# A hand-written planner counts small products for half of TensorE's load and lets blocks of TensorE instructions come later

## The chip, the cores and the metric

The kernel runs on one core of a Trainium2 chip. The metric is device time in microseconds (us) of one execution, the median of several. Engines are named as in the profile: PE (TensorE matmuls), PEld (its weight loads), DVE (VectorE), ACT (ScalarE), POOL (GpSimd), SP (the queue that issues the transfers).

## The reference, cut to what matters

Three stages follow each other on 4 batches of 768 tokens: a gated recurrent attention (8 heads of 40), a token mixer whose weights are a 768 x 768 matrix pair, and a gated convolution.

```
for t in range(S):                                   # attention, S = 768
    m_new = maximum(f_gate + m, i_gate); f_stab, i_stab = exp(f_gate+m-m_new), exp(i_gate-m_new)
    C = f_stab * C + i_stab * outer(v, k);  n = f_stab * n + i_stab * k
    y[t] = sigmoid(o_gate) * (C @ q) / maximum(abs(n @ q), 1)
theta = x @ w_theta                                  # x: y as (4, 768, 320)
y = w_tok_r @ (x * cos(theta)) + w_tok_i @ (x * sin(theta))
u = x + y;  x2 = u + maximum(u @ w_ch, 0)
out = (sigmoid(conv5(x2)) * (x2 @ w_val)) @ w_out
```

## The kernel before

**Attention** works in 12 groups g of two chunks of 128 tokens (`attend`, once per group). On PE a group is `weigh` (28 bf16 matmuls that build the decay exponents in two banks of PSUM; ACT takes their Exp into a tile W), `scores` (k by q, in the same two banks; DVE multiplies them into W), `carry` (twice 32, the state's update), `numer` (64, W by v) and `inter` (64, state by q). A float32 matmul counts as two PE matmuls, each with its weight load, so a group has 284. Their outputs are 41, 64 or 128 to 512 columns wide. `finish` on DVE divides and applies the output gate, whose Sigmoid (`sig`, tiles `x_m`) runs on ACT for two groups at a time. Exp, Sigmoid and Sin need different tables on ACT, so a change of function costs an `ACT_TABLE_LOAD`.

**The mixer and the convolution** are 24 steps. `theta` makes x @ w_theta and its sine and cosine for 128 tokens (tiles `th_m`, `z`); `weight` converts one block of the token matrix (tiles `r_b`, `wt_m`); `mix` adds 30 products of 384 columns per block; the `f_...` functions are the rest. `theta` for the first 128 tokens comes in the program between the last groups of attention, because it takes the same two banks.

**Conversions.** The dense weights come as float64 bit patterns, and `cv_piece` turns each of 13 pieces (three each of w_theta, w_ch, w_val and w_out, and the convolution's) into float32: one Abs on ACT, then four operations on DVE in place in `xT_m` (`cv_bits`: two TENSOR_SCALAR, two SCALAR_TENSOR_TENSOR), then a split into a high and a low part (`out_hi`, `out_lo`, `val_hi`, `val_lo`) on ACT and on DVE or POOL. Nothing needs the w_val and w_out pieces before the convolution stage.

**The order of the work** is not the program's. Every call is recorded as a step of a `Plan`, with engines that may do it and a cost for each; `order` then simulates the engines and takes, whenever an engine is free, the ready step that is due first. For PE it keeps a model of the clock and of the instruction stream (`array`): time is cut into windows, the share of work in a window switches the modelled clock between half and full speed (to full above WARM, back to half below COLD), and every BLOCK = 127 matmuls a new block of instructions begins, no earlier than FETCH us after the block before it began. `issue` runs `order` four times, each time with PE's due times taken from the run before, keeps the run that its own model ends first, and records the instructions in that order. Each engine then runs its list strictly in that order.

Of the kernel before, what the change touches and what calls it, by code (L numbers as in the profile page):

```python
# [72 lines left out]
class Plan:  # L73
# [8 lines left out]
    LATE, AGAIN, BESIDE = -2.5, 4, 0.5  # L82
    HOP, TABLE, HOLD = 0.15, 1.3, 5.0
    WINDOW, PHASE, WARM, COLD = 3.413, 0.6, 0.85, 0.45
    BLOCK, FETCH = 127, 3.6
    DMA_ISSUE, DMA_START, DMA_END, DMA_RATE, DMA_DEPTH = 0.475, 0.65, 0.95, 260e3, 8

    def __init__(self, nc):
# [108 lines left out]
    def order(self, aim=None):  # L197
        steps, after = self.steps, self.edges()
# [26 lines left out]
        def array(n, t):  # L225


            nonlocal slow, window, worked, used, block
            cost, todo = steps[n]["cost"]["pe"], steps[n]["ninst"]
            load, each = min(1.0, steps[n]["work"] / cost), cost / todo  # L230
            while todo:
                some = min(todo, self.BLOCK - used)
                left = some * each
                while left > 1e-6:
                    w = int((t + self.PHASE + 1e-6) / self.WINDOW)
                    for _ in range(window, w):
                        share, worked = worked / self.WINDOW, 0.0
                        slow = share < (self.WARM if slow else self.COLD)
                    window = w
                    rate = 0.5 if slow else 1.0  # L240
                    span = min(left / rate, (w + 1) * self.WINDOW - self.PHASE - t)
                    left -= span * rate
                    worked += span * load
                    t += span
                todo -= some
                used += some
                if used == self.BLOCK:
                    t, used = max(t, block), 0
                    block = t + self.FETCH
            return t  # L250
# [41 lines left out]
        for _ in count:  # L292
# [8 lines left out]
            when, n = best[u]  # L301
# [6 lines left out]
            if u == "sp":  # L308
                flight = [e for e in flight if e > when]
                if len(flight) >= self.DMA_DEPTH:  # L310
                    when = sorted(flight)[-self.DMA_DEPTH]
                free[u] = when + self.DMA_ISSUE
                dma = max(dma, free[u] + self.DMA_START) + s["bytes"] / self.DMA_RATE
                end = dma + self.DMA_END
                flight.append(end)
            else:
                if s["table"] not in (None, table):
                    table, when = s["table"], when + self.TABLE
                end = free[u] = array(n, when) if u == "pe" else when + s["cost"][u]
                if locks(n, u):  # L320
                    port = end
# [802 lines left out]
```

## Time and profile before

| what | before |
|---|---|
| median of 3 runs | 422.21 us (422.06 to 422.3) |
| the profiled execution: its time, its span | 419.87 us, 418.2 us |
| busy share of the span: PE, DVE, ACT, POOL | 89%, 79%, 51%, 16% |
| mean granted TensorE clock | 0.89 of full |

The span is from the first to the last instruction; the execution's time is 1.7 us more. The profiled execution is 2.3 us below the median. By the names of the tiles the span has four parts: start and gates (0 to 18 us), attention (18 to 135), the start of the mixer, in which the tail of attention, the first thetas and the first mixes lie together (135 to 179, called the transition here), and the mixer and the convolution (179 to the end).

### The profile page before, as it was taken

To read this page: it belongs to the slowest core of one execution; us is meant where nothing else is said; L and a number is where in the kernel's file an instruction comes from. 1 tells how busy PE (TensorE), PEld (TensorE's weight loads), DVE (VectorE), ACT (ScalarE), POOL (GpSimd) and SP (SyncE) were. 2 spreads that over 40 slices of the span, in tenths; PEclk is the share of its full clock that TensorE was granted. 3 is DMA by queue.
4 is the path that set the end of the run, shared out by engine and by line. 5 is a ranking of instruction groups with operands and counts; after the bars stand their busy time and mean duration, and the time that the engine had idled before them with its cause. 6 is when DMAs were issued, how large, how long until landed. Compare 5 with 4: busy or idle time off the path is not lost.

```text
span 418.2 us, 11566 instructions
## 1 busy us (share of the span) xinstructions
PE 371.0 (89%) x4828; PEld 341.0 (82%) x4828; DVE 329.2 (79%) x673; ACT 212.5 (51%) x359; POOL 67.9 (16%) x83
## 2 busy tenths in 40 slices
PE   5696985758699787999999999999999999999986
PEld 4585884657587666879999989999799999999975
DVE  7874797678768899999999987469937449667992
ACT  2660515432524978587554375655684324144644
POOL 2211314122244201000110210010010002021500
PEclk9566579597757798999999999999999999999998
DMA  6896679666869659677672067320330530000202
GB/s 178 244 229 184 215 200 244 195 218 186 266 183 265 195 166 297 214 245 266 247 256 108 11 233 274 139 75 12 106 102 15 195 122 0 2 0 2 95 2 94
DMA packets 29300, 65.63 MB, mean 157 GB/s; under 512 B 5216, under 2 KB 14592, under 8 KB 29248
## 3 DMA queue, kind: packets, MB, share of 16 engines
q1 hardware_dynamic: 29248, 64.90, 49.4%
q8 instruction: 38, 0.62, 0.6%
q14 instruction: 14, 0.11, 0.1%
HBM read 47.58 MB, written 17.30 MB: 155 GB/s over the span
## 4 chain that ended last, share of the span: by engine, by line
PE 49%; DVE 22%; issue 6%; ACT 5%; POOL 0%; DVEq 0%; ACTq 0%
PE bank L67 49%; DVE k_m L67 10%; DVE r_b L67 2%; ACT th_m L67 2%; DVE th_m L67 2%; DVE xT_m L67 1%; DVE hl_z L67 1%; DVE wt_m L67 1%; DVE z L67 1%; DVE f_m L67 1%; DVE num_m L67 1%; ACT xT_m L67 1%; DVE sr_f L67 1%; ACT r_b L67 0%; ACT L67 0%
## 5 line engine op out<-in xcount | busy, mean ns | idle before, releaser
L67 PE MATMUL bank<-wt_m,z 128*128 128x384 f32 x480 | 91.2, 346 | 3.3 <-DVE z L67 1.3
L67 PEld LDWEIGHTS bank<-wt_m,z 128*128 128x128 f32 x480 | 84.9, 191 | 5.8 <-DVE wt_m L67 1.6
L67 DVE SCALAR_TENSOR_TENSOR k_m<-k_m,cw_sb,k_m 128x384 f32<-128x384 f32 x76 | 44.8, 641 | 0.4
L67 PE MATMUL bank<-w_t,xT_m 128*128 128x320 f32 x144 | 42.2, 443 | 2.8 <-ACT xT_m L67 2.8
L67 PE MATMUL bank<-w_r,z 128*128 128x384 f32 x240 | 44.3, 340 | 0.0
L67 PEld LDWEIGHTS bank<-w_r,z 128*128 128x128 f32 x240 | 41.6, 188 | 0.5
L67 PEld LDWEIGHTS bank<-w_t,xT_m 128*128 128x128 f32 x144 | 27.2, 193 | 14.1 <-ACT xT_m L67 4.2
L67 ACT ACTIVATE W<-bank 128x512 f32<-128x512 f32 x24 | 14.3, 597 | 34.8 <-PE bank L67 34.5
L67 DVE TENSOR_TENSOR k_m<-k_m,bank 104x164 f32<-104x164 f32 (+1 forms) x36 | 15.0, 420 | 21.1 <-PE bank L67 17.8
L67 PE MATMUL bank<-k_m,q_m 40*64 40x41 f32 x384 | 18.1, 273 | 7.6 <-issue 7.6
L67 PE MATMUL bank<-r_b,W 64*64 64x41 f32 x768 | 21.5, 284 | 2.8 <-issue 2.8
L67 PE MATMUL bank<-q_m,k_m 40*64 40x64 f32 x768 | 19.5, 265 | 4.9 <-issue 2.6
L67 PEld LDWEIGHTS bank<-r_b,W 64*64 64x64 f32 x768 | 19.9, 198 | 4.2 <-issue 3.9
L67 ACT ACT_TABLE_LOAD x18 | 23.1, 1283 | 0.5 <-DVE W L67 0.2
L67 DVE SCALAR_TENSOR_TENSOR r_b<-r_b,r_b 128x768 int32<-128x768 int32 x24 | 22.8, 951 | 0.4
L67 PE MATMUL bank<-r_b,kw_m 64*40 64x41 f32 x704 | 16.6, 234 | 7.2 <-issue 5.8
L67 ACT ACTIVATE th_m<-th_m 128x640 f32<-128x640 f32 (+1 forms) x27 | 19.0, 702 | 7.1 <-DVE th_m L67 6.7
L67 DVE TENSOR_TENSOR W<-W,bank 128x512 f32<-128x512 f32 x24 | 15.7, 679 | 8.3 <-PE bank L67 8.2
L67 PEld LDWEIGHTS bank<-q_m,k_m 40*64 40x64 f32 x768 | 17.4, 175 | 5.6 <-issue 2.9
L67 PEld LDWEIGHTS bank<-k_m,q_m 40*64 40x64 f32 x384 | 15.2, 184 | 8.0 <-issue 4.6
L67 PEld LDWEIGHTS bank<-r_b,kw_m 64*40 64x40 f32 x704 | 13.9, 145 | 9.0 <-issue 6.8
L67 ACT ACTIVATE th_m<-bank,magic 128x320 f32<-128x320 f32 x24 | 12.6, 524 | 16.7 <-PE bank L67 9.0
(168 smaller groups left out, 851.0 us busy)
## 6 DMA issues: line engine op xcount, KB each, us to landing
r_b<-in_wtok_dram SPq DMA_DIRECT2D x24, 384.0 KB
wt_dr<-wt_m SPq DMA_DIRECT2D x12, 768.0 KB
w_r<-wt_dr SPq DMA_DIRECT2D x8, 768.0 KB
r_b<-in_v_dram SPq DMA_DIRECT2D x12, 328.0 KB
q_m<-in_qT_dram SPq DMA_DIRECT2D x24, 160.0 KB
k_m<-in_kT_dram SPq DMA_DIRECT2D x24, 160.0 KB
r_b<-in_kt_dram SPq DMA_DIRECT2D x12, 320.0 KB
x_m<-in_og_dram SPq DMA_DIRECT2D x24, 160.0 KB
```

Of the source, the lines that this page charges most:

```text
L67: calls[u] = lambda e=e: getattr(e, op)(*args, **kw)
```

## The change

Two numbers of the planner's PE model change, and nothing in the computation. A PE step whose matmuls are modelled at under 0.06 us each counts with half its load when the share of work in a window is summed. Those are all steps of `weigh`, `scores`, `carry`, `numer` and `inter`, and a small one in `gate_unit`; the steps of `theta`, `mix` and the convolution are modelled at 0.11 us or more. Half is below WARM, so in the new model a stretch of attention alone never gets the full clock. And FETCH goes from 3.6 to 4.2 us.

```
-    BLOCK, FETCH = 127, 3.6
+    BLOCK, FETCH = 127, 4.2
...
-            load, each = min(1.0, steps[n]["work"] / cost), cost / todo
+            each = cost / todo
+            load = min(1.0, steps[n]["work"] / cost) * (0.5 if each < 0.06 else 1.0)
```

With the old numbers `issue` keeps the first of its four runs, with the new ones the third. PE's list of mixes, thetas and convolution is the same from the fifth block of the first mix on, but for one exchange of neighbours; in attention every engine has another list.

The first place is on DVE, in the transition. This is DVE's list before; `xT_m` is a conversion of a w_val or w_out piece, `th_m` and `x_m_82` are theta, `r_b` is the token matrix:

```order
L67 TENSOR_SCALAR xT_m_91<-xT_m_91 128x320
L67 TENSOR_TENSOR x_m_80<-x_m_80,num_m 128x640
L67 TENSOR_SCALAR xT_m_91<-xT_m_91 128x320
L67 TENSOR_TENSOR out_lo<-xT_m_91,out_hi 128x320
L67 SCALAR_TENSOR_TENSOR xT_m_91<-xT_m_91 128x320
L67 SCALAR_TENSOR_TENSOR r_b_86<-r_b_85,r_b_86 128x768
L67 SCALAR_TENSOR_TENSOR xT_m_91<-xT_m_91 128x320
L67 TENSOR_SCALAR xT_m_91<-xT_m_91 128x320
L67 SCALAR_TENSOR_TENSOR th_m<-th_m,bank_101 128x320
L67 TENSOR_SCALAR xT_m_91<-xT_m_91 128x320
L67 TENSOR_TENSOR th_m<-th_m,x_m_82 128x640
```

Five pieces stood there. Now the last of the thirteen ends three groups before attention does. This is DVE's list now, around the product of W for group 7:

```order
L67 TENSOR_SCALAR xT_m_91<-xT_m_91 128x320 x2
L67 SCALAR_TENSOR_TENSOR xT_m_91<-xT_m_91 128x320
L67 TENSOR_TENSOR W<-W,bank_101 128x512
L67 TENSOR_TENSOR W<-W,bank_102 128x512
L67 TENSOR_TENSOR k_m_88<-k_m_88,bank_107 104x164
L67 TENSOR_SCALAR xT_m_91<-xT_m_91 128x320
L67 SCALAR_TENSOR_TENSOR xT_m_91<-xT_m_91 128x320
L67 TENSOR_SCALAR xT_m_91<-xT_m_91 128x320
L67 TENSOR_TENSOR num_m<-bank_105,ewc 128x8x41
L67 SCALAR_TENSOR_TENSOR xT_m_91<-xT_m_91 128x320
```

All 20 in-place operations of the five pieces have moved into attention, the three `out_lo` and one of the two `val_hi` have gone to POOL there.

The second place is on ACT, at the last group. Before, with W the two Exps of `weigh` and `x_m` the last Sigmoids; the third load is the one for Sin:

```order
L67 ACTIVATE W<-bank_101 128x512
L67 ACT_TABLE_LOAD
L67 ACTIVATE x_m_79<-x_m_79 128x640
L67 ACTIVATE x_m_80<-x_m_80 128x640
L67 ACT_TABLE_LOAD
L67 ACTIVATE W<-bank_102 128x512
L67 ACTIVATE xT_m_91<-xT_m_91 128x320
L67 ACTIVATE wt_m_109<-r_b_86 128x768
L67 ACT_TABLE_LOAD
```

And now:

```order
L67 ACTIVATE W<-bank_101 128x512
L67 ACTIVATE r_b_86<-r_b_84 128x768
L67 ACTIVATE W<-bank_102 128x512
L67 ACT_TABLE_LOAD
L67 ACTIVATE x_m_79<-x_m_79 128x640
L67 ACTIVATE x_m_80<-x_m_80 128x640
L67 ACT_TABLE_LOAD
L67 ACTIVATE th_m<-th_m 128x640 x2
```

The two Sigmoids have moved behind both Exps, and one of the three loads is gone. Elsewhere in attention the Sigmoids of four groups are put together twice; in all ACT's list has 14 table loads where it had 19.

## Rows read from the trace of the kernel before

**Rows 1.** The page's heading.
```profile
span 418.2 us, 11566 instructions
```
**Rows 2.** Windows by stage: stretch, its length, busy us (instructions), PEclk, DMA share, GB/s.
```profile
18.00:135.00 117.00, 91.00 (x3101) 80.33 (x3094) 86.79 (x236) 45.46 (x76) 33.81 (x46) 0.70 0.76 217
135.00:179.00 44.00, 35.89 (x341) 30.21 (x341) 42.48 (x82) 34.74 (x57) 4.33 (x5) 0.88 0.70 222
179.00:240.00 61.00, 60.91 (x341) 58.39 (x339) 59.30 (x98) 34.73 (x51) 6.25 (x4) 1.00 0.53 186
240.00:400.00 160.00, 158.51 (x901) 151.78 (x900) 114.99 (x195) 81.39 (x142) 20.24 (x17) 1.00 0.26 90
400.00:419.00 19.00, 12.83 (x64) 11.08 (x62) 10.22 (x20) 8.21 (x17) 0.00 (x0) 0.91 0.14 53
```
**Rows 3.** Waits of PE in 18:135, its largest: us, times, longest.
```profile
PE bank L67 <- issue: 21.2, 14, 3.6
```
**Rows 4.** The chain of waits in 70:94, a part: start us, us, what.
```profile
72.19 3.58 issue
75.77 7.82 PE bank L67 x252
...
84.79 3.09 PE bank L67 x128
87.88 1.18 issue
89.06 2.05 PE bank L67 x122
```
**Rows 5.** The page's DMA queues: packets, MB, share.
```profile
q8 instruction: 38, 0.62, 0.6%
```
**Rows 6.** Waits of DVE in 18:135, the two largest.
```profile
DVE W L67 <- PE bank L67: 7.6, 6, 2.6
DVE num_m L67 <- PE bank L67: 6.5, 5, 2.3
```
**Rows 7.** Waits of PE in 135:179, the three largest.
```profile
PE bank L67 <- ACT xT_m L67: 2.4, 2, 1.4
PE bank L67 <- ACT W L67: 2.3, 1, 2.3
PE bank L67 <- DVE z L67: 1.3, 1, 1.3
```
**Rows 8.** Timeline of ACT in 134:144, a part: start us, us, what.
```profile
135.18 1.28 ACT L67 ACT_TABLE_LOAD   x1
136.48 1.36 ACT L67 ACTIVATE x_m<-x_m 128x640 f32<-128x640 f32 x2
137.86 1.28 ACT L67 ACT_TABLE_LOAD   x1
139.15 0.60 ACT L67 ACTIVATE W<-bank 128x512 f32<-128x512 f32 x1
```
**Rows 9.** Groups of DVE by shape in 135:179: xcount, busy us, mean ns, idle before.
```profile
L67 DVE SCALAR_TENSOR_TENSOR xT_m<-xT_m 128x320 int32<-128x320 int32 x10 | 4.9, 485 | 0.1
L67 DVE TENSOR_SCALAR xT_m<-xT_m 128x320 f32<-128x320 f32 x5 | 1.9, 372 | 0.5 <-ACT xT_m L67 0.4
L67 DVE TENSOR_SCALAR xT_m<-xT_m 128x320 int32<-128x320 int32 x5 | 1.6, 318 | 0.0
L67 DVE TENSOR_TENSOR out_lo<-xT_m,out_hi 128x320 fp32r<-128x320 f32 x3 | 1.4, 481 | 0.0
L67 DVE TENSOR_TENSOR val_hi<-xT_m,val_hi 128x64 fp32r<-128x64 f32 x2 | 0.6, 284 | 0.0
```
**Rows 10.** Windows of the two stretches of the transition at the low clock.
```profile
140.00:147.00 7.00, 6.23 (x134) 5.24 (x129) 6.00 (x13) 6.91 (x12) 2.55 (x2) 0.51 0.79 238
164.00:168.00 4.00, 3.86 (x13) 3.87 (x14) 4.00 (x10) 3.52 (x7) 0.00 (x0) 0.57 0.72 253
```

## The prediction

> **What bounds the kernel now.** I read the windows by stage first, since an average over the span hides four different limits. From 179 us on PE is the bound: it is busy 60.91 of 61 us, then 158.51 of 160 us, at the full clock [rows 2]. Its list there is the same in both programs but for two exchanges of neighbours, so whatever the change does has to be won or lost before 179 us, and then everything behind shifts by that much. The last 19 us, with PE busy 12.83, are a tail of dependent pieces, which I take as shifted too.
>
> In attention, 18 to 135 us, no engine is full: PE is busy 91.0 of 117 us at a mean granted clock of 0.70, DVE 86.8, ACT 45.5 [rows 2]. Who is late there is told by the waits. PE's largest wait by far is "issue", 21.2 us in 14 pieces [rows 3]: PE sat still and no other engine had held it. The chain of waits shows where these pieces fall. A pause of 3.58 us is followed by 252 matmuls, and after the next pause come 128 and, after another, 122 [rows 4]; the queue that brings instructions moved 38 packets [rows 5], and the kernel's 4828 matmuls over 38 are 127 in a packet. So the pauses stand at the edges of blocks of 127 matmuls: PE has emptied one block and the next has not come. Two blocks in a row began at 84.79 and 89.06 us, 4.27 us apart [rows 4]; that is the pace at which blocks can come, as long as PE finishes each sooner. The stage's 3101 matmuls are 24.4 blocks in 117 us, 4.8 us a block. Attention therefore runs close to this pace and DVE follows PE: its two largest waits there are for PE [rows 6], and it has 117 - 86.8 = 30.2 us of idle time.
>
> In the transition, 135 to 179 us, it is the other way round. DVE is busy 42.48 of 44 us, PE 35.89 [rows 2], and PE waits for DVE and ACT in turn [rows 7].
>
> **The change part by part.**
>
> *The numbers themselves.* FETCH of 4.2 us is nearer to the 4.27 us that the chain shows than 3.6 was. Half load keeps the planner's clock low through attention, where the granted clock is 0.70 on average [rows 2]; neither full nor half is right, but with both numbers the plan is of a slow PE in attention, as the trace has it. None of this changes a duration; it moves work.
>
> *Conversions out of the transition.* Five pieces leave it: 10 SCALAR_TENSOR_TENSOR at 485 ns, 10 TENSOR_SCALAR at 372 and 318 ns, 3 out_lo at 481 and 2 val_hi at 284 ns, by their groups 4.9 + 1.9 + 1.6 + 1.4 + 0.6 = 10.4 us of DVE [rows 9]. DVE's 42.5 us become 32.1, and it stops being full. PE then needs its 35.89 us of work, less what it loses at the low clock: two stretches at 0.51 and 0.57 hold 6.23 and 3.86 us of busy time [rows 10], which at the full clock would be about 6.23 x 0.51 + 3.86 x 0.57 = 5.4 us, 4.7 us less. So the transition can give at most its PE idle time, 44 - 35.89 = 8.1 us, and these 4.7 us: 12.8 us. At least it can give nothing, if PE's waits lie in the chain of theta (PE to ACT to DVE to ACT to DVE and back to PE for mix) and not in DVE's load.
>
> *One table load and the Sigmoids.* The second Exp of the last group waited while ACT loaded a table (1.28 us), did two Sigmoids (1.36 us) and loaded the first table back (1.28 us) [rows 8], and PE waited 2.3 us for it [rows 7]. Now the Exps come first. That wait of 2.3 us, part of the 8.1, should go. Five fewer loads in all spare ACT 5 x 1.28 = 6.4 us, of which I count nothing else: ACT is busy 45.5 of 117 us in attention.
>
> *My value for the transition.* Of 12.8 us the 2.3 are named; of the other 10.5 I take about 4, because theta's chain keeps some of PE's waits (2.4 us of them are for ACT's copies of xT_m [rows 7], which are not moved) and with the waits some of the low clock may stay. Together -6.4 us, half of the bound.
>
> *Conversions into attention.* The 20 in-place operations and one val_hi, 4.9 + 1.9 + 1.6 + 0.3 = 8.7 us of DVE, now stand between attention's own. The cover is DVE's 30.2 us of idle time there; without it they would cost 8.7 us. An operation of 0.3 to 0.5 us in DVE's list delays what is queued behind it, the product of W and the sums of numerators, for which PE waits. But PE has pauses of up to 3.6 us, 14 in all [rows 3], that such a delay can fall into. The pieces' transfers, five of 128 x 320 64-bit words (0.33 MB each, 1.64 MB), go through SP's queue earlier; at 217 GB/s they are 7.6 us of transfer time, against a DMA share of 0.76, that is 28 us not in use. I count nothing for them. Several state products change places between DVE and POOL, both ways; I count nothing for these too.
>
> *PE's new order in attention.* A group is now the same sequence almost throughout: weigh, carry, numer, scores, carry, inter. It cannot beat the pace of blocks: 24.4 x 4.27 = 104 us, 12.8 us below the 117. At the other end it costs the 8.7 us above. I take zero, near the present state, because the same 284 matmuls per group pass the same limit.
>
> *Sum.* 419.9 - 6.4 = 413.5 us for an execution like the profiled one, whose span was 418.2 us [rows 1]; the median of the runs is 2.3 us higher, so 415.8, rounded to **416 us**.
>
> **The rivals.**
>
> *The cover in attention is not there* (slower). If DVE's idle time lies only at moments when PE has nothing for it anyway, each moved operation pushes the W products back and PE with them. Fully uncovered the move costs 8.7 us and the transition returns 6.4: 422.2 + 8.7 - 6.4 = 424.5 us; with the transition's gain down to the 2.3 us, 428.6. It decides when more than 6.4 of the 8.7 us, three quarters, are paid. For it: in windows of attention DVE is busy 74% on average, so each of the 12 groups has only some 30.2 / 12 = 2.5 us free. Against it: DVE's waits are for PE, and PE's are for instructions.
>
> The same rival has a second source. If the pauses named issue were not instruction blocks, the plan's 4.2 us per block would fill attention with DVE work on the strength of a pause that a better order might have closed; PE's busy time and its other waits would be 117 - 21.2 = 95.8 us, and DVE's 86.8 + 8.7 = 95.5 us would be level with it, with no room for chains. The Trainium skill, page "Runtime: NRT & Kernel Launch", section "Instruction fetch mechanics", speaks for that: it says that instructions are refilled in 16 KiB blocks of 256 and that crossing a block is mostly hidden. The trace agrees on the block (127 matmuls with 127 weight loads) but not on the hiding, with 21.2 us of pauses at the edges. I give that source 0.03 of this rival's chance.
>
> *The transition is bound by theta's chain* (little change). DVE's load falls and PE still waits for the same copies and products. Only the 2.3 us go: 419.9 us. For it: PE's largest wait there is for ACT's copies [rows 7]. Against it: those copies waited behind conversions' Abs and high parts on ACT, which leave with the pieces.
>
> *Attention gets quicker as well.* A regular sequence spreads weigh, the slowest part per matmul, evenly over the blocks. A quarter of the 12.8 us with the transition's gain gives 412.6 us, a half 409.4.
>
> **How the numbers follow.** Forecast, 412 to 418 us: 0.44. Quicker attention, below 412: 0.17. Chain-bound transition, 418 to 423: 0.16, of which 0.07 lie within 0.2% (421.4 to 423.1, about what measurement can tell from no change here). Lost cover, above 423: 0.23. So faster 0.70, same 0.07, slower 0.23. The range leaves out the fully paid move with no gain behind it and a quicker attention beyond half of its bound: 409 to 425 us; the likeliest case alone has 412 to 418.
>
> **What would show it.** Right: no conversion of w_val or w_out in the transition; DVE's busy share in attention up from 74% to some 82%, attention's last scores no later than now; PE dense at the full clock 5 to 8 us sooner than 179; no PE wait of over 2 us for ACT's W there; the part behind unchanged in length. Wrong: if attention ends 5 us or more later, with PE waiting for DVE at W or num_m; if the pauses named issue grow beyond 21 us; or if the part behind 179 us changes its length, which I hold for impossible within 1 us, since PE is full there.

## The result: slower, where faster was forecast

The changed kernel takes 422.97 us (median of 20 runs, 418.1 to 427.77), the kernel before 417.86 us (20 runs, 415.16 to 422.3). The ratio is 1.0113, with a 95% interval of 1.0083 to 1.0144: 4.7 us slower. The forecast was 416 us, 6.2 us below the 422.21 us that stand for the kernel before ahead of the prediction. Those were the median of three high runs, the highest of the twenty. So the 2.3 us that the forecast's sum adds at its end have the wrong sign: by the 20 runs the profiled execution of the kernel before lies 2.0 us above the median. Ratios here leave out runs that lie over 1.5% above the fastest of their kernel, so they can differ a little from what two medians give.

The profiled execution of the changed kernel took 425.05 us, with a span of 423.3, and is 5.2 us longer than the one profiled before. By stage it answers to [rows 2]; columns as there:

```profile
18.00:135.00 117.00, 98.52 (x2959) 86.56 (x2955) 94.48 (x237) 42.60 (x80) 42.62 (x58) 0.57 0.80 225
135.00:179.00 44.00, 37.83 (x425) 31.20 (x426) 37.15 (x65) 28.74 (x46) 3.24 (x3) 0.84 0.62 195
179.00:240.00 61.00, 60.13 (x337) 57.83 (x335) 57.09 (x89) 34.52 (x51) 4.71 (x3) 1.00 0.53 190
240.00:400.00 160.00, 158.89 (x900) 151.62 (x901) 114.92 (x196) 82.79 (x143) 23.11 (x18) 1.00 0.26 89
400.00:424.00 24.00, 16.88 (x89) 15.43 (x87) 14.60 (x28) 9.00 (x19) 0.00 (x0) 0.89 0.15 53
```

In attention PE is busy 98.5 us instead of 91.0, with 142 products fewer, at a mean granted clock of 0.57 instead of 0.70. DVE is busy 94.5 us. PE's waits there, which answer to [rows 3]:

```profile
PE bank L67 <- issue: 12.8, 8, 3.6
PE bank L67 <- DVE num_m L67: 3.1, 4, 1.7
PE bank L67 <- DVE f_m L67: 1.3, 2, 1.0
PE bank L67 <- DVE W L67: 0.7, 2, 0.4
```

The pauses for instructions fell from 21.2 to 12.8 us, and still attention got longer.

**The two programs at equal products.** Fixed stretches mix a different amount of work, so I cut both spans at the same numbers of PE's products. The 1270th, the 2794th and the 3810th, counted from 0, start at 61.4, 117.7 and 230.0 us before, and at 63.9, 126.0 and 233.6 us now. The windows between them, before:

```profile
61.40:117.70 56.30, 38.80 (x1537) 34.09 (x1533) 41.61 (x113) 23.27 (x36) 15.08 (x22) 0.78 0.75 219
117.70:230.00 112.30, 102.69 (x1028) 92.54 (x1023) 105.81 (x200) 71.42 (x112) 16.99 (x18) 0.90 0.68 223
```

And the changed kernel:

```profile
63.90:126.00 62.10, 54.43 (x1534) 48.04 (x1534) 53.13 (x126) 21.05 (x37) 27.21 (x38) 0.50 0.82 240
126.00:233.60 107.60, 99.70 (x1030) 90.06 (x1022) 95.95 (x162) 66.65 (x100) 8.88 (x8) 0.92 0.59 198
```

The second stretch, the transition and what follows, is 4.7 us shorter. The first, attention, is 5.8 us longer: the same number of products keeps PE busy 54.4 us at a clock of 0.50 throughout, where it was 38.8 us at 0.78. That is 15.6 us more of PE's busy time, against some 10 us of waits saved (17.6 us of PE's waits in that stretch before, 7.5 now). Ahead of it 2.5 us were lost, and 1.5 us behind it.

### The profile page after: what moved, and what is told of

Same layout as the page of the kernel before. It is cut to its first block, busy times and chain, and to the rows that moved or that the text cites. A ratio compares the mean times of both kernels' runs of the same rounds, so it can differ in the third digit from the quotient of the medians.

```text
span 423.3 us, 11574 instructions
## 1 busy us (share of the span) xinstructions
PE 385.0 (91%) x4828; PEld 352.8 (83%) x4828; DVE 333.6 (79%) x658; ACT 206.1 (49%) x357; POOL 77.2 (18%) x95
## 4 chain that ended last, share of the span: by engine, by line
PE 56%; DVE 27%; issue 6%; DMA 5%; ACT 4%; SPq 0%; POOL 0%; DVEq 0%; ACTq 0%
PE bank L67 56%; DVE k_m L67 11%; DMA xT_m<-in_w_ch_dram 3%; DVE th_m L67 2%; DVE f_m L67 2%; DVE num_m L67 2%; DVE r_b L67 2%; DVE xT_m L67 2%; DMA r_b<-in_wtok_dram 1%; DVE hl_z L67 1%; DVE g_m L67 1%; ACT th_m L67 1%; DVE wt_m L67 1%; DVE W L67 1%; DVE sr_f L67 1%
## 5 line engine op out<-in xcount | busy, mean ns | idle before, releaser
L67 PE MATMUL bank<-wt_m,z 128*128 128x384 f32 x480 | 88.3, 341 | 0.2 <-DVE wt_m L67 0.2
L67 PEld LDWEIGHTS bank<-w_t,xT_m 128*128 128x128 f32 x144 | 28.5, 202 | 12.3 <-issue 1.8
L67 PE MATMUL bank<-q_m,k_m 40*64 40x64 f32 x768 | 23.8, 293 | 7.2 <-ACT W L67 3.6
L67 PEld LDWEIGHTS bank<-q_m,k_m 40*64 40x64 f32 x768 | 21.9, 202 | 7.6 <-ACT W L67 3.7
L67 PE MATMUL bank<-r_b,W 64*64 64x41 f32 x768 | 23.9, 294 | 2.9 <-DVE num_m L67 2.9
L67 PE MATMUL bank<-k_m,q_m 40*64 40x41 f32 x384 | 20.7, 276 | 6.0 <-issue 6.0
L67 PEld LDWEIGHTS bank<-r_b,W 64*64 64x64 f32 x768 | 22.0, 208 | 4.4 <-DVE num_m L67 3.4
L67 PEld LDWEIGHTS bank<-k_m,q_m 40*64 40x64 f32 x384 | 18.2, 188 | 6.3 <-issue 6.2
L67 PE MATMUL bank<-r_b,kw_m 64*40 64x41 f32 x704 | 20.5, 260 | 1.6 <-DVE f_m L67 1.3
L67 DVE TENSOR_TENSOR th_m<-th_m,x_m 128x640 f32<-128x640 f32 x22 | 17.4, 819 | 5.1 <-ACT th_m L67 5.0
L67 ACT ACTIVATE f_m<-bank 64x384 f32<-64x384 f32 x16 | 7.8, 486 | 28.1 <-PE bank L67 27.9
```

Of the source, the lines that this page charges most:

```text
L67: calls[u] = lambda e=e: getattr(e, op)(*args, **kw)
```

## The experiments

Three theories stood at first. **T1**: the moved conversions hold up PE through DVE. **T2**: PE's new list in attention keeps its clock at the lower level, and PE itself is slower. **T3**: in the last group a block of the token matrix stands ahead of an Exp and makes PE wait. Each kernel was compared with the kernel before on the same chip.

| kernel | ratio to before | 95% interval | PE busy, DVE busy, clock in 18:135 |
|---|---|---|---|
| before | 1 | | 91.0, 86.8, 0.70 |
| changed | 1.0113 | 1.0083 to 1.0144 | 98.5, 94.5, 0.57 |
| FETCH alone | 1.0101 | 1.0047 to 1.0154 | 99.7, 90.2, 0.56 |
| half load alone | 0.9953 | 0.9919 to 0.9987 | 85.2, 95.1, 0.74 |
| changed, no in-place operations | 1.0126 | 1.0054 to 1.0197 | 101.0, 91.5, 0.62 |
| before, no in-place operations | 1.0047 | 1.0007 to 1.0086 | 91.8, 84.3, 0.68 |
| changed, no pieces | 1.0061 | 1.0019 to 1.0104 | 90.8, 87.8, 0.69 |

**Each number alone.** One kernel has only the first line of this diff, the other only the second.

```
-    BLOCK, FETCH = 127, 3.6
+    BLOCK, FETCH = 127, 4.2
...
+            load = min(1.0, steps[n]["work"] / cost) * (0.5 if each < 0.06 else 1.0)
```

> Only FETCH = 4.2, small products at full load. Fewer conversions are moved into attention, and PE's list there is near that of before. T1 (moved conversions hold up PE through DVE): half of the loss or less, ratio to before 1.000 to 1.006. T2 (the new order of PE's list in attention keeps the granted clock low): no loss, ratio 0.995 to 1.002, granted clock in attention near the 0.70 of before. T3 (ACT's Abs of the token matrix between the last two Exps): only a loss if that Abs stands there too.

> Only the half load, FETCH = 3.6. All conversions stand in attention, as in the changed kernel. T1: the loss is there, ratio to before 1.008 to 1.014. T2: the loss is there if PE's list in attention is as regular as in the changed kernel, with a granted clock in attention of 0.57 to 0.60; a clock near 0.70 with the loss all the same speaks against T2.

Measured: 420.74 us with FETCH alone, ratio 1.0101, and 415.24 us with half load alone, ratio 0.9953. The whole loss comes with the 4.2, with only two of the five pieces moved; the half load, with all five moved, is 2 us faster than before. T1 said the opposite of both. FETCH alone has the low clock, half load alone the high one, as T2 has it for a loss and no loss; but T2 missed too, since it expected a clock near 0.70 and no loss from FETCH alone. The two numbers do not simply add up: 4.2 us lost and 2.0 won would make 2.2, and together they lose 4.7, though the intervals are too wide to be sure of the difference. Attention of FETCH alone, and of half load alone, in stretches of the same products as above:

```profile
66.70:124.40 57.70, 49.16 (x1535) 43.17 (x1531) 47.42 (x128) 21.45 (x34) 15.21 (x21) 0.59 0.80 228
```

```profile
65.20:122.60 57.40, 43.01 (x1534) 37.66 (x1532) 50.35 (x134) 21.98 (x38) 21.40 (x33) 0.71 0.82 243
122.60:225.30 102.70, 97.34 (x1018) 88.26 (x1015) 97.64 (x163) 64.62 (x100) 10.21 (x9) 0.95 0.61 210
```

The half load's attention takes 57.4 us, 1.1 us longer than before, although its clock is nearly as high. Its gain lies behind: 102.7 us for the stretch that took 112.3.

**The in-place operations left out.** All lists stay as they are; the 20 DVE operations on the five pieces are not issued.

```
         for n in best[1]:
+            if self.steps[n]["leave"]:
+                continue
```

> The changed kernel, every engine's list as it is, without the 20 in-place operations of DVE on the five pieces that the change moved into attention (that part of the conversion is left out, so five weight pieces hold wrong numbers). 8.4 us of DVE leave attention. T1: attention's last scores come 5 us or more sooner, the time falls by 6 to 9 us, to 414 to 417. T2: PE's pace in attention is set by its clock, the time falls by 0 to 2 us, to 421 to 423. T3: the same, 421 to 423.

> The kernel before, every engine's list as it is, without the same 20 in-place operations, which stand in the transition here (the same part is left out). DVE is less full there: if the transition is bound by DVE, as the forecast has it, the time falls by 4 to 8 us, to 410 to 414; if theta's chain binds it, by 0 to 2. Against the run of the changed kernel without these operations: T1 makes the two equal within 2 us, T2 and T3 leave that one 6 to 11 us longer, all of it before the first mix.

Measured: 420.89 us (ratio 1.0126) and 419.85 us (1.0047). In the changed kernel nothing that the interval can tell came back, and the 414 to 417 us of T1 did not come. But this interval is wide, 1.0054 to 1.0197, and by the medians the kernel is 3.3 us above the kernel before, where the changed kernel is 5.1 us above: up to 2 us may have come back. Its profiled execution did run attention's products in 56.8 us, but it was the fastest of its six runs (415.62 to 424.3). In the kernel before, the transition lost these operations and the time did not fall; it came out 0.5% longer, which no theory expected and no run explains. DVE's load was not what bound it.

**The tail's exchange on ACT, and more products on PE.** In the first kernel the Abs of the token matrix comes behind both last Exps. Two others repeat the first products of `weigh`, in every group or in one, and the fourth is the changed kernel unchanged, in another execution. The numbers are the planner's steps: 676 is the second Exp, 822 the Abs, 823 the first DVE operation behind it.

```
+        for n in (822, 823):
+            order.remove(n)
+        at = order.index(676) + 1
+        order[at:at] = [822, 823]
...
+            plan.steps[-1]["extra"] = [lambda o=G_ps[half(u)]: tc.nc.tensor.matmul(
+                o, past, eye.unsqueeze(1).to_broadcast([128, 8, U]), start=True, stop=True)
+                for u in range(2)] * 1
```

> The changed kernel, with one exchange on ACT: in the last group the Abs of the token matrix comes behind both Exps instead of between them. T3 (that Abs, waiting for its transfer, makes PE wait 3.6 us): the wait of PE for ACT's W falls below 1 us, the first mix comes 3 us sooner, the time falls by 2 to 4 us, to 419 to 421. T2: what is lost lies ahead of it, in attention; the tail gets 0 to 2 us shorter, 421 to 423.

> The changed kernel, every list as it is, with 4 more products per group on PE: the first two products of each half of weigh, 512 columns, are done twice (the second overwrites the first, the result is the same). 48 products, 0.21 us each at the full clock and 0.43 at half: 10 to 20 us more work for PE, more columns in a row in each group. T2 (what costs the time is that the clock stays at half through attention, and PE's own pace there with it): the granted clock in attention rises from 0.57 to 0.70 or more and the time does not rise by the added work: 415 to 423. If PE's work or instructions in attention are the limit and the clock is only a by-product: 432 to 443.

> The same in one group alone: 8 more products of 512 columns in weigh of group 5, at about 68 us, 1.7 to 3.4 us of added work. T2: the clock goes to full there; it and the places of the later groups differ from there on, time 419 to 423, that is no longer than without the burst. If the clock is a by-product: 425 to 427, the clock at half from 60 to 120 us as before.

> The changed kernel once more, another execution. T2: where the granted clock of attention in this execution differs from 0.57, its end moves with it, a higher clock with an earlier end, while DVE's and ACT's work is the same; with the clock at 0.57 attention ends where it did, 5 us later than before.

Measured: 423.23 us (1.0114) with the exchange; 423.18 us (1.0102) with 48 more products; 422.51 us with the burst, where the twelve runs spread from 416.77 to 426.94 and settle nothing; 422.29 us for the changed kernel once more. The exchange took away PE's wait for ACT and left one of 4.4 us for DVE's W in its place, so T3 in that form fell.

The 48 products are the telling ones. The first row is all of PE in attention, the second the 40 added products that fall into it, the third the kernel's own:

```profile
18.00:135.00 117.00, 93.83 (x3017) 78.60 (x3007) 96.74 (x240) 42.29 (x80) 43.84 (x59) 0.69 0.80 225
18.00:135.00 117.00, 12.28 (x40) 3.20 (x40) 0.69 0.80 225
18.00:135.00 117.00, 88.77 (x2977) 77.86 (x2967) 96.60 (x239) 38.36 (x69) 43.84 (x59) 0.69 0.80 225
```

PE took on 12.3 us of work in this stage at no cost in time. The clock rose from 0.57 to 0.69, and the kernel's own products kept PE busy 88.8 us instead of 98.5 (some of the added ones run beside them). It is not the one execution alone: the clock of the whole span was 0.886 to 0.906 in all six runs, with a mean of 0.897, and 0.846 to 0.894 in the twenty of the changed kernel, with a mean of 0.868. So what PE's list holds does move its clock, and the clock is worth some 10 us of PE's busy time here. But the time did not fall either. This is no clean price of the clock, since the added products also stand ahead of each group's Exp.

In the second execution of the changed kernel the clock was 0.64 and PE's busy time 95.2 us, and attention ended sooner, as T2 expected of a higher clock. But it won back only 1.9 of the 5.8 us:

```profile
62.50:122.70 60.20, 50.21 (x1531) 43.62 (x1527) 52.19 (x126) 21.08 (x37) 25.55 (x38) 0.62 0.83 235
```

A higher clock by itself has not given attention back in any of these; T2 is a part at most.

**PE's list of before, and a first try at the tail.** In one kernel PE has the list of before up to the last group's `weigh`, with all other lists those of the changed kernel. In two others the block of the token matrix comes behind the last group's products of W, with and without the in-place operations; in these two the next transfer into the tile comes ahead of the conversion, so that another block is converted, which costs time of its own (the mended order further on is some 4 us shorter). The fourth is the kernel before, with the last two Sigmoids (step 606) behind the last Exp.

```
+        order.remove(606)
+        at = order.index(676) + 1
+        order[at:at] = [606]
```

> The changed kernel, but the Abs and the four DVE operations on the third block of the token matrix come behind the last group's two Exps and its two products of W, not ahead of them. T3, wider than at first (with the Abs moved alone, PE waited 4.45 us for DVE's product of W, since the four operations still stood ahead of it): both waits of PE go, 3.6 us for ACT and 1.8 us for DVE, the stretch from theta's first transposes to its second falls from 18.3 us to about 14, the time falls by 4 to 5 us, to 418 to 420. If the block is needed soon after, it comes back as a wait of mix: 422 to 424.

> The changed kernel, all lists of DVE, ACT, POOL and SP as they are, but PE's list in attention, up to the last group's weigh, is that of the kernel before. T2 (PE's order keeps the clock at half): granted clock in attention 0.68 or more, theta's first transposes 4 to 5 us sooner, at 128 to 129 us, time 417 to 420. T1 (DVE's and ACT's lists): attention no shorter, 422 to 425, or longer, where PE now waits for what DVE does in another order.

> The same as the last but one (block of the token matrix behind the last products of W), and without the 20 in-place operations on the five moved pieces (that part of the conversion is left out). Against that run the difference is what those 8.4 us of DVE cost in attention. T1: 4 us or more, 413 to 415. T2: 0 to 2 us, 416 to 419.

> The kernel before, with one exchange on ACT: the last two Sigmoids, with the table load that they need, come behind the last group's second Exp, as the change has them. The forecast counted 2.3 us for it: 415.5. If the end of the product of W, and not the Exp, sets when theta goes on, it is 0 to 1 us: 417 to 418.

Measured: 427.67 us (1.0209), 456.37 us (1.0897), 427.19 us (1.0198), 420.14 us (0.9999; the kernel before took 420.16 on this chip). PE's old list under the new lists of the others is 36 us longer, with PE waiting for DVE at every kind of product, so it tells nothing of T2: an engine's list can't be judged apart from the others'. The first and third carry the late transfer in both, and differ by 0.5 us.

The last one prices a step of the forecast. With the Sigmoids moved, PE's wait of 2.3 us for ACT's W is gone, and these stand in its place in the transition (the wait for z was 1.3 us before [rows 7]):

```profile
PE bank L67 <- DVE W L67: 5.5, 1, 5.5
PE bank L67 <- DVE z L67: 2.3, 1, 2.3
```

**The tail mended, the opposite exchange, and the pieces left out whole.** The conversion of the token matrix's block (822 to 826), with the next transfer (886) behind it, comes after the last products of W (678, 679); the half-load kernel gets the opposite order; and the changed kernel is run without the transfers, Abs and DVE work of the five pieces.

```
+        order[719:734] = [
+            675, 676, 822, 944, 606, 677, 678, 660, 699, 679, 823, 824, 825, 826, 886,
+        ]
...
+        plan.leave = (nm, k_) in LEAVE
         sp.dma_start(out=raw, in_=src if nm == "cw" else src[:, k_ * DM:(k_ + 1) * DM])
         cv_abs(raw, v)
         cv_bits(raw, v)
+        plan.leave = False
```

> The changed kernel with the last group's two Exps and two products of W ahead of the Abs and the four DVE operations on the third block of the token matrix, and the next transfer into that block's tile kept behind them. T3: PE's waits for W, 3.6 and 1.8 us, go, theta's second transposes come 4 to 6 us sooner, the time falls by 4 to 5 us, to 418 to 420. If mix needs the block soon after: 422 to 424.

> The same, and without the 20 in-place DVE operations of the five moved pieces (that part of the conversion is left out). T1: 4 us or more below the run with them. T2: 0 to 2 us below it.

> The half-load kernel (415.2) with the opposite exchange: Abs and DVE operations on the third block of the token matrix ahead of the last group's second Exp and of both products of W, as the changed kernel has them. T3: theta's second transposes come 3 to 5 us later, 418 to 420. If the tail has room there: 415 to 416.

> The changed kernel, every list as it is, without the transfer, the Abs and the 20 DVE operations of the five moved pieces (their high and low parts are still made, from what lies in the tile). T1 in its wide form (transfers, ACT and DVE of the moved pieces): 1.64 MB, 4 us of ACT and 8.4 us of DVE leave attention, its products from the 1270th to the 2794th take 56 us, the time falls by 5 us or more, to 418 or less. T2 (PE's own list and clock): they take 59 to 62 us still, 421 to 423.

Measured: 422.16 us (1.0106), 422.32 us (1.0083), 416.44 us (0.9954) and 421.02 us (1.0061). The tail's order is worth nothing that can be told, in either direction: the half-load kernel with the bad order is as fast as with the good one. In the mended kernel PE's waits for W are down to 1.3 us, 0.9 for DVE and 0.4 for ACT, and ACT's copies are late instead; PE's waits in 133:170:

```profile
PE bank L67 <- ACT xT_m L67: 2.4, 1, 2.4
PE bank L67 <- issue: 2.3, 1, 2.3
PE bank L67 <- DVE W L67: 0.9, 1, 0.9
```

Without the five pieces the ratio falls from 1.0113 to 1.0061, some 2 us, with intervals that overlap. Both engines are lighter in attention then (DVE 87.8 us, PE 90.8 at a clock of 0.69), and still it is slower than before. The stretch of attention's products took 56.8 us, as T1 had it, no longer than the 56.3 of before; but the time that T1 drew from it, 418 us or less, did not come:

```profile
66.10:122.90 56.80, 49.19 (x1535) 42.80 (x1534) 42.15 (x105) 18.76 (x33) 25.14 (x38) 0.62 0.81 234
```

This execution began the stretch at 66.1 us, 4.7 later than the kernel before. So not all that is lost is lost in one place.

**The Sigmoids earlier.** Behind the last Exp ACT's list has a table load, two Sigmoids and another load before theta's Sin. Here the Sigmoids stand ahead of group 10's Exps, which spares one load, without and with the mended order of the tail. The theory, **T4**, is that ACT's chain of Exp, loads, Sigmoids, Sin and copies sets when the mixes begin. ACT's list against that of the changed kernel:

```
-L67 ACTIVATE W<-bank_101 128x512
-L67 ACT_TABLE_LOAD
+L67 ACTIVATE x_m_79<-x_m_79 128x640
+L67 ACTIVATE x_m_80<-x_m_80 128x640
+L67 ACT_TABLE_LOAD
+L67 ACTIVATE W<-bank_101 128x512
...
-L67 ACT_TABLE_LOAD
-L67 ACTIVATE x_m_79<-x_m_79 128x640
-L67 ACTIVATE x_m_80<-x_m_80 128x640
```

> The changed kernel, but the Sigmoids of the last four groups stand together ahead of group 10's two Exps (as in the half-load kernel), not between these and behind the last Exp: on ACT 1.36 us of Sigmoids and one table load of 1.28 us leave the stretch between the last Exp and theta's Sin. T4 (ACT's chain of Exp, tables, Sigmoids, Sin and copies sets when the mixes begin): first mix 2 to 4 us sooner, 419 to 421. If PE's pace alone sets it: 422 to 423.

> The same, and the third block of the token matrix behind the last products of W. T4: with both out of ACT's and DVE's way the tail is that of the half-load kernel, first mix 4 to 7 us sooner, 416 to 419. If not more than the Sigmoids alone give: as that run.

Measured: 421.11 us (1.0095, 1.0057 to 1.0133) and 421.34 us (1.0101, 1.0052 to 1.0149). By these ratios some 0.5 to 1 us of the 4.7 lies in the tail, less than the intervals can tell from nothing.

The profiled executions by their lists, without those with added products:

| lists of | 1270th | 1270th to 2794th | 2794th to 3810th | behind |
|---|---|---|---|---|
| before (3 kernels) | 61.4 to 63.1 | 54.8 to 56.3 | 112.3 to 114.7 | 188.0 to 189.3 |
| changed, all work, small exchanges (6) | 62.5 to 65.5 | 56.7 to 62.8 | 105.5 to 108.1 | 188.2 to 189.8 |
| changed, no in-place operations or no pieces (3) | 61.6 to 66.1 | 55.0 to 56.8 | 105.8 to 107.9 | 189.7 to 189.8 |
| half load alone (2) | 65.2, 62.6 | 57.4, 56.3 | 102.7, 105.1 | 189.1, 189.8 |
| FETCH alone (1) | 66.7 | 57.7 | 103.8 | 191.3 |

The three profiled executions of before's lists lie 1 to 4 us above the medians of their own kernels, so these columns show where the time goes, not its sum to the microsecond. In the third row two of the three are the fastest run of their kernel, and in the second the one with the shortest attention, 56.7 us, is too. Within the second row the clock of this stretch does not order its length: 0.50, 0.55, 0.56, 0.59, 0.62 and 0.64 go with 62.1, 62.8, 59.2, 56.7, 60.2 and 61.9 us. In the third row is neither of the two kernels with the late transfer; the one of them without in-place operations needed 61.3 us for attention's products.

## Why the prediction was wrong

**PE's new order in attention: counted at zero, and the stage got about 5 us longer.** This is the step that failed. The zero rested on "the same 284 matmuls per group pass the same limit", the 4.27 us per block, "as long as PE finishes each sooner". At the clock that the old list got, 127 products were 38.80 / 1537 x 127 = 3.2 us of PE's time. At the half level they are 54.43 / 1534 x 127 = 4.5 us, and PE no longer finishes sooner. Of the new numbers the text said that "none of this changes a duration". The durations did change: under the new lists PE was granted a lower clock, and each product took longer. For at least 60 of the stage's 117 us PE was held at the lower level, 1.2 GHz:

```profile
60.00:120.00 60.00, 52.61 (x1513) 46.89 (x1509) 54.21 (x129) 19.26 (x36) 27.86 (x39) 0.50 0.86 246
```

That the loss comes with the lists made with 4.2, and not with the moved conversions as such, is shown by the half load: DVE is as busy there (95.1 us), all five pieces are moved, PE was busy 85.2 us in the stage instead of 98.5, and nothing was lost. But FETCH alone, which loses nearly as much as both numbers together, took 57.7 us for the products for which the half load took 57.4; in its profiled execution the time went ahead of them, where 66.7 us stand for 61.4, and behind. So where the 4.2 costs its time is not the same in both kernels. That the clock alone makes the loss is not shown: PE's same list ran at 0.50 and at 0.62 and was slow both times, and with the added products the clock was high and the time no shorter.

The prediction's own first sign of being wrong came. These are attention's last scores, before and now:

```profile
139.80 1.73 PE L67 MATMUL bank<-q_m,k_m 40*64 40x64 f32 x62 [2.34 <-ACT W L67]
148.70 1.52 PE L67 MATMUL bank<-q_m,k_m 40*64 40x64 f32 x62 [3.60 <-ACT W L67]
```

They start 8.9 us later. But the waits that the sign named with it, PE's for DVE at W or num_m, hardly grew: 3.8 us in 18:135 instead of 3.2.

The Trainium skill, page "Runtime: NRT & Kernel Launch", section "Instruction fetch mechanics", says that crossing an instruction block is mostly hidden. The pauses of 12.8 us in this stage, which again lie multiples of 127 products apart to within 3, say that it still is not; that they are fewer than the 21.2 us of before fits a slower PE, which comes to the edges later.

**Conversions into attention: covered, counted at zero.** The operations themselves cost little: leaving them out gave nothing by the ratio in one comparison (1.0126 against 1.0113, with an interval of 3 us to either side) and 1 us in the other (1.0083 against 1.0106). The pieces as a whole, with transfers and ACT's part, cost about 2 us. What was mis-sized is their price. The groups of DVE in 18:135 of the changed kernel, count, busy us and mean ns:

```profile
L67 DVE SCALAR_TENSOR_TENSOR xT_m<-xT_m 128x320 int32<-128x320 int32 x24 | 18.1, 755 | 0.2
L67 DVE TENSOR_SCALAR xT_m<-xT_m 128x320 int32<-128x320 int32 x12 | 5.2, 435 | 0.2
L67 DVE TENSOR_SCALAR xT_m<-xT_m 128x320 f32<-128x320 f32 x12 | 3.7, 319 | 2.0 <-ACT xT_m L67 1.9
```

And the first of these in the kernel before:

```profile
L67 DVE SCALAR_TENSOR_TENSOR xT_m<-xT_m 128x320 int32<-128x320 int32 x14 | 6.9, 490 | 0.0
```

The forecast moved ten of them at 485 ns each; all twenty-four now average 755 ns, the fourteen that stood there before among them, 18.1 us instead of 6.9 + 4.9. POOL is busy 42.6 us in that stage instead of 33.8, and the dear ones are all among those that ran beside its work: the six that ran while POOL was idle took 474 to 481 ns, the eighteen that ran beside a POOL operation 847 ns on average. Before, ten of the fourteen ran while POOL was idle.

**The rival "cover in attention is not there"** had the sign, a chance of 0.23 and a time, 424.5 us, close to the measured one. Its first mechanism, moved operations that push the W products back, is not what the runs show. Its second remark comes nearer: PE and DVE level with each other "with no room for chains". PE is busy 98.5 and DVE 94.5 of 117 us, and each waits for the other. But PE's waits for DVE there, 5.1 us in the rows of the result, were 4.7 us before, and the half load lost nothing with DVE as busy, so a full DVE alone is not the cause. PE's waits for DVE in 18:135 of the kernel before:

```profile
PE bank L67 <- DVE W L67: 2.4, 3, 1.7
PE bank L67 <- DVE k_m L67: 1.5, 2, 0.8
PE bank L67 <- DVE num_m L67: 0.8, 1, 0.8
```

Two full engines would fit what the experiments gave: DVE made lighter returned 0 to 2 us, PE's clock made higher returned the added work and no more, both made lighter by leaving out the pieces returned 2. This is argued, not shown by a run that frees both without leaving work out.

**One table load and the Sigmoids: counted 2.3 us, measured 0.** With the two Sigmoids moved in the kernel before the ratio is 0.9999 (0.9959 to 1.0039). The Sigmoids and a load stay in ACT's list, only later, and PE waits 5.5 us for DVE's W instead. In the changed kernel the planner put a new wait in the same place, which answers to [rows 7, 8]. ACT from the last Exps on:

```profile
143.03 0.60 ACT L67 ACTIVATE W<-bank 128x512 f32<-128x512 f32 x1 [0.32 <-PE bank L67]
147.28 0.89 ACT L67 ACTIVATE r_b<-r_b 128x768 f32<-128x768 f32 x1 [3.65 <-DMA r_b<-in_wtok_dram]
148.07 0.58 ACT L67 ACTIVATE W<-bank 128x512 f32<-128x512 f32 x1
148.67 1.28 ACT L67 ACT_TABLE_LOAD   x1
149.96 1.36 ACT L67 ACTIVATE x_m<-x_m 128x640 f32<-128x640 f32 x2
151.33 1.28 ACT L67 ACT_TABLE_LOAD   x1
```

and PE's two largest waits in 135:179:

```profile
PE bank L67 <- ACT W L67: 3.6, 1, 3.6
PE bank L67 <- DVE W L67: 1.8, 1, 1.8
```

An Abs that nothing needed soon stood at the head of ACT's list and waited for its transfer. It looked like a cause, and the exchanges showed that what it hides costs as much.

**The transition: -6.4 us, measured -4.7** in the pair of profiles, and -4 to -9 between the first two rows of the table. The size was near, the reason was not right: relieving DVE of the in-place operations, with before's lists, shortened nothing (113.6 us for the stretch instead of 112.3). It is the new lists that do it; which of their exchanges does is not shown, and that the size came near is luck.

**The part behind 179 us** was to keep its length within 1 us. From theta's sixth transposes (184.1 us before, 187.8 now) to the end it went from 234.1 to 235.5 us. Executions with the same lists differ there by as much (188.2 to 189.8 us in the last column), so nothing follows from it.

**What stays open.** Why the plans made with 4.2 keep PE at the lower level, and those made with 3.6 less so, was not settled, nor where FETCH alone loses its 4 us, nor how attention's 5 us divide between PE's clock, the dearer DVE operations and the moved transfers. For the clock there is an estimate: among the twenty runs of the changed kernel a higher clock goes with a shorter time, some 0.7 us for 0.01, though loosely (correlation -0.42). Its mean of 0.868 against 0.886 in 109 runs of the kernel before would then be worth about 1.3 of the 4.7 us. Half load alone is the version that beats both kernels, by 0.5% against before.

## What to carry to other kernels

A list that keeps PE denser can be slower: PE was busy 98.5 us instead of 91.0 in attention, with fewer products. Compare PE's busy time for an equal number of products and the granted clock beside it, before counting saved pauses as a gain. Two numbers of a planner that are changed together are to be timed apart; here one alone lost 4 us, the other alone won 2, and both together lost 4.7. A wait named in a profile is worth its length only if nothing else in the waiting chain is as late, and moving one instruction in one list is a cheap way to see that.

## What was not expected of the hardware

PE can be busy all the time and still be held at the lower of its two levels. Three stretches of the changed kernel's attention, PE's busy time first and the granted clock third from the end:

```profile
70.00:75.00 5.00, 5.00 (x188) 4.93 (x187) 4.93 (x10) 0.79 (x2) 3.74 (x5) 0.50 0.94 242
85.00:90.00 5.00, 5.00 (x131) 4.12 (x122) 4.61 (x10) 3.50 (x6) 3.55 (x5) 0.50 0.69 209
110.00:115.00 5.00, 5.00 (x152) 4.48 (x152) 5.00 (x15) 2.13 (x4) 0.72 (x1) 0.50 0.91 227
```

With 40 products of 512 columns added to this stage its mean clock was 0.69, and the kernel's own products then kept PE busy 10 us less. Executions of one program differ in this too: the changed kernel's attention had 0.57 in one and 0.64 in another.

The same DVE operation, 128 x 320 in place, took 490 ns on average in one attention stage and 755 ns in another in which POOL was busier, 42.6 us instead of 33.8. Beside a POOL operation a single one took up to 1997 ns; in the attention stages of all the traces here, 167 of them ran while POOL was idle, and none of these took over 493 ns.
